# Two-layer decode attention with a feed-forward block: streaming the values past the probabilities in four column groups, and two lists of deferred steps

## The chip, the cores and the metric

The kernel runs on one core of one Trainium2 chip. The metric is device time in microseconds (us) of one execution. Before the change the median of three runs is 663.71 us (663.58 to 664.17). Matrix work is done by TensorE (PE; its weight loads are listed as PEld), elementwise work by VectorE (DVE), ScalarE (ACT) and GpSimd (POOL). SyncE (SP) issues every load from device memory (HBM). SBUF is the on-chip memory of 128 partitions, and PSUM holds the eight banks that TensorE writes into.

## The reference

One token per sequence (`Sq = 1`), four sequences, `D = 512`, 32 query heads on 8 key/value heads of `Dh = 128`, caches of `Sk = 8192` positions, bf16. The same attention and feed-forward block is applied twice, with the same weights and caches:

```python
def _A_ref(x, k_cache, v_cache, wq, wo):
    q = (x @ wq).reshape(B, 1, 32, 128).transpose(0, 2, 1, 3)
    k, v = jnp.repeat(k_cache, 4, axis=1), jnp.repeat(v_cache, 4, axis=1)
    p = softmax(einsum("bhqd,bhkd->bhqk", q, k) * 128 ** -0.5)
    o = einsum("bhqk,bhkd->bhqd", p, v)
    return o.transpose(0, 2, 1, 3).reshape(B, 1, 32 * 128) @ wo
def _B_ref(x, w_gate, w_up, w_down):
    return (silu(x @ w_gate) * (x @ w_up)) @ w_down
x = A_x
for _ in range(2):
    x = x + _A_ref(layernorm(x), ...)
    x = x + _B_ref(layernorm(x), ...)
```

A layer's K and V caches have 2 MB for each pair of sequence and key/value head, 64 such blocks of K and V together, and 128 MB in all.

## The kernel before, in words

**Units.** One unit `u` is a pair of key/value head `g = u // 4` and sequence `b = u % 4`, so there are 32 units in each layer. For a unit, four query heads (`REP = 4`) meet 8192 positions. A 2 MB block of K or V lies in one of eight slots of `kvf`: partition `p` holds positions `64 p` to `64 p + 63`, cut into eight blocks `q` of eight positions (`NB = 8`, `TB = 8`).

**Scores.** `turn` (line 389) turns each block of K in place on VectorE, as 32-bit words in 32x32 squares. `scores` (line 409) then runs four matmuls of 256 columns for each block, 32 for a unit, with the queries (`zq`) as weights. `place_q` (line 400, GpSimd) writes the next unit's queries into `zq`.

**Softmax.** Five steps follow a unit's last scores: `max_p` (line 415, VectorE), `max_t` (lines 419, 422, 425: PE, VectorE, ScalarE), `exps` (lines 431, 435, 437, 439: PE, then ScalarE), `turn_p` (line 442, VectorE: the probabilities turned into `pT`) and `total` (lines 445 and 447: the sum and its reciprocal `rl`).

**Values.** `values` runs 64 matmuls for a unit (line 495): each has 128x128 of V as weights and 32 columns of probabilities streaming past, of which the first four are wanted (the others fall into columns that nobody reads). `scale_o` (line 503) multiplies by `rl`. After the four units of a head group, `out_proj` (lines 524 to 534) applies `wo` and adds to `x`.

**What sets the order.** The program is unrolled in Python, and each engine executes its own instructions in the order in which they were written. `keys` and `values` append blocks to a list `blocks` with a nominal length each; `drain` keeps about 2 us of them waiting, so VectorE's turns are written ahead of the matmuls that need them. The steps behind softmax and values stand in one list, `line`; `advance` takes a block's nominal length off the first step's gap and writes the step down once its gap is used up. `flush(u)` writes down everything up to the last step of unit `u`. `values` puts its own `rest` (`scale_o`, then perhaps `out_proj`) in front of the list.

**Layers and loads.** Layer 0 takes units 0 to 31; layer 1 takes 29, 30, 31 first, whose K and V are still in slots 0 to 5 from layer 0 and whose K is already turned, and then 0 to 28. In a layer the order is K of a unit, then V of the unit before it; the last three V come at the end. SyncE issues loads in a fixed list (`items`), each as soon as a slot is free (`finished`, `pump`). At a layer's end the feed-forward weights `w_gate`, `w_up`, `w_down` are loaded into slots 6 and 7 and a spare strip; K and V of layer 1 can go there only when `ffn` (lines 602 and 619) has read them. `halves` reloads the slots of K of units 29 and 30 in two halves as their scores get done.

Of the kernel before, what the change touches and what calls it, by code (L numbers as in the profile page):

```python
# [5 lines left out]
ACTF = mybir.ActivationFunctionType  # L6
# [97 lines left out]
def bass_interleave_layers__gqa_block_cached__swiglu_ffn__decode_kernel(  # L104
# [24 lines left out]
    TB = 8  # L129
# [8 lines left out]
    NQ = 4  # L138
    NSLOT = 8
    NKEEP = 6  # L140
    WIDE = 32
# [4 lines left out]
    with ExitStack() as es:  # L146
# [32 lines left out]
        xx = sb("xx", [P, XB], FP32)  # L179
        lnv = sb("lnv", [P, B], FP32)  # L180
        rstd = sb("rstd", [P, B], FP32)
        xc = sb("xc", [P, XB], FP32)
        xn = sb("xn", [P, XB], BF16)
        oT = sb("oT", [P, Hq, B], BF16)
# [6 lines left out]
        pT = sb("pT", [P, 2, SW + WIDE], BF16)  # L191
        qT = pT[:, 1, 0:XQ].rearrange("p (b h) -> p b h", b=B)
        rl = sb("rl", [P, 2, REP], FP32)
        xoT = sb("xoT", [P, XB], BF16)
# [42 lines left out]
        for a in range(NA):  # L237
# [6 lines left out]
        T.op("dve", lambda e: e.memset(pT[:, :, SW:], 0.0), writes=["pT0", "pT1"])  # L244
        T.op("dve", lambda e: e.tensor_reduce(head[:], identf[:].rearrange("p (x h) -> p h x", h=REP), AX.X, ALU.max),
             reads=["ident"], writes=["head"])
        nc.scalar.preload_act_table_set("natural_log_exp_and_others")
# [4 lines left out]
        turn_of = {}  # L252

# [116 lines left out]

        def advance(us):
            if line:
                line[0][0] -= us
                while line and line[0][0] <= 0:
                    line.pop(0)[2]()

        def flush(tag=None):
            while line and (tag is None or any(s[1] == tag for s in line)):
                line.pop(0)[2]()
# [61 lines left out]
        def turn_p(u):  # L441
            T.op("dve", lambda e: e.transpose(pT[:, turn_of[u], 0:SW], pb[:]), reads=["pb"], writes=[f"pT{turn_of[u]}"])  # L442

        def total(u):
            T.op("pe", lambda e: e.matmul(bank(TOT)[:, 0:REP], lhsT=ones, rhs=rsm[:], start=True, stop=True),  # L445
                 reads=["rsm", "onesf"], writes=[f"pb{TOT}"])
            T.op("dve", lambda e: e.reciprocal(rl[:, turn_of[u], :], bank(TOT)[:, 0:REP]), reads=[f"pb{TOT}"],  # L447
                 writes=[f"rl{turn_of[u]}"])
# [35 lines left out]
        def values(L, u):  # L484
# [3 lines left out]
            def block(q):  # L488
                if q == 0:
                    flush(u)  # L490
                s = slot_of["V", L, u]

                for t in range(q * TB, (q + 1) * TB):
                    c0 = (t % TB) * QB + REP * q
                    T.op("pe", lambda e: e.matmul(bank(bk)[:, 0:WIDE], lhsT=kv[:, s, t * Dh:(t + 1) * Dh],  # L495
                                                  rhs=pT[:, turn_of[u], c0:c0 + WIDE], start=(t == 0), stop=(t == TT - 1)),
                         reads=[f"s{s}.{q}", f"pT{turn_of[u]}"], writes=[f"pb{bk}"], sig=(t % TB == TB - 1))
                if q == NB - 1:
                    finished(("V", L, u))
                    line[0:0] = rest  # L500

            def scale_o():
                T.op("dve", lambda e: e.tensor_tensor(oT[:, g * REP:(g + 1) * REP, b], bank(bk)[:, 0:REP],  # L503
                                                      rl[:, turn_of[u], :], ALU.mult),
                     reads=[f"pb{bk}", f"rl{turn_of[u]}"], writes=["oT"])

            rest = [[0.3, None, scale_o]]
# [3 lines left out]
            blocks.extend((0.2, lambda q=q: block(q)) for q in range(NB))  # L511
# [6 lines left out]
        def out_proj(g):  # L518
# [3 lines left out]
            for c in range(REP):  # L522
                for h in range(REP):
                    T.op("pe", lambda e: e.matmul(ob[h * QB:(h + 1) * QB, c, :], lhsT=pick[:, c, :],
                                                  rhs=oT[:, g * REP + h, :], start=True, stop=True),
                         reads=["oT", "ident"], writes=[f"pb{OUTB}"], sig=(h == REP - 1))
# [13 lines left out]
        def center():  # L540
# [8 lines left out]
            T.op("dve", lambda e: e.scalar_tensor_tensor(bk3(xc[:]), total, -1.0 / D, bk3(xT[:]),  # L549
                                                         op0=ALU.mult, op1=ALU.add),  # L550
                 reads=["x", f"pb{LNB}"], writes=["xc"])
            T.op("dve", lambda e: e.tensor_tensor(xx[:], xc[:], xc[:], ALU.mult), reads=["xc"], writes=["xx"])
            T.op("dve", lambda e: e.tensor_reduce(vs[:], xx[:].rearrange("p (k b) -> p b k", b=B), AX.X, ALU.add),
                 reads=["xx"], writes=["vs"])
# [147 lines left out]
```

## Time and profile before

| what | value |
| --- | --- |
| median of three runs | 663.71 us |
| the profiled execution's own time | 665.22 us |
| its span, first to last instruction | 663.3 us |
| mean granted TensorE clock | 0.816 |
| busy: PE, PEld, DVE, ACT, POOL | 509.0, 400.4, 382.7, 101.4, 19.3 us |
| moved by DMA | 275.00 MB, mean 415 GB/s |
| instructions | 17301 |

The profile's page has the busy time of each engine, the span in 40 slices, the DMA queues, the chain of work that ended last, the costliest groups of instructions (source line, engine, operation, output <- input, shapes, count, busy time, mean duration of one, and the idle time of the engine just before them with what ended it) and the DMA issues. From the trace behind it one can ask for a table of any stretches of time, and for the instructions in order of time. Clock 1.00 is TensorE at full speed. A busy share near 1 for DMA means that the mean of the 16 DMA engines had work all the time.

### The profile page before, as it was taken

How to read it: one execution, taken by the hardware profiler on the slowest of the kernel's cores; microseconds unless marked ns; L12 is line 12 of the kernel's file. 1: busy time of each engine (PE TensorE's matmuls, PEld its weight loads, DVE VectorE, ACT ScalarE, POOL GpSimd, SP SyncE). 2: the span in 40 equal slices, each digit the busy share in tenths (PEclk: the TensorE clock that was granted, in tenths of full speed). 3: DMA queues.
4: the chain of work that ended last, by engine and by line, in shares of the span. 5: the costliest groups of instructions: out<-in, count | busy, mean ns of one | idle time of the engine just before them, and what ended most of it. 6: DMA issues, size and time to landing. Idle time of an engine off the chain costs nothing.

```text
span 663.3 us, 17301 instructions
## 1 busy us (share of the span) xinstructions
PE 509.0 (77%) x7656; PEld 400.4 (60%) x7656; DVE 382.7 (58%) x897; ACT 101.4 (15%) x331; POOL 19.3 (3%) x73
## 2 busy tenths in 40 slices
PE   1767786877877777886976999878778797686796
PEld 0555565655656655665665878756556575465675
DVE  1646475575566565574732289766466566465562
ACT  0011111110111111110110212111111111011120
POOL 0000000000000000000000000000000000000000
PEclk9997788876879869788775979977788877688885
DMA  9999999999999999999998999999999999999995
GB/s 370 426 424 414 433 430 423 424 428 425 428 426 424 427 427 426 426 423 428 424 404 350 387 396 428 425 427 427 425 426 426 426 426 428 428 424 426 427 413 208
DMA packets 24107, 275.00 MB, mean 415 GB/s; under 512 B 2392, under 2 KB 2400, under 8 KB 7904
## 3 DMA queue, kind: packets, MB, share of 16 engines
q1 hardware_dynamic: 24032, 273.89, 98.2%
q8 instruction: 60, 0.98, 0.6%
q14 instruction: 15, 0.12, 0.0%
HBM read 273.88 MB, written 0.00 MB: 413 GB/s over the span
## 4 chain that ended last, share of the span: by engine, by line
DMA 68%; PE 23%; SPq 5%; DVE 2%; issue 2%; POOL 0%; DVEq 0%; POOLq 0%
DMA kvf<-in_A_k_cache_dram 63%; PE ps L409 14%; DMA kvf<-in_B_w_down_dram 5%; PE ps L495 5%; SPq L93 5%; PE ps L431 1%; PE ps L445 1%; DVE kvf L389 1%; PE ps L568 1%; DVE pT L442 0%; PE ps L419 0%; PE ps L619 0%; PE ps L530 0%; DVE rl L447 0%; PE ps L581 0%
## 5 line engine op out<-in xcount | busy, mean ns | idle before, releaser
L389 DVE STREAM_TRANSPOSE kvf<-kvf 128x512 f32<-128x512 f32 x488 | 313.1, 677 | 187.7 <-DMA kvf<-in_A_k_cache_dram 187.6
L409 PE MATMUL ps<-kvf,zq 128*128 128x256 bf16 x2048 | 332.1, 319 | 9.1 <-DVE kvf L389 6.5
L409 PEld LDWEIGHTS ps<-kvf,zq 128*128 128x128 bf16 x2048 | 215.5, 113 | 69.0 <-DVE kvf L389 10.1
L495 PEld LDWEIGHTS ps<-pT,kvf 128*128 128x128 bf16 x4096 | 119.8, 97 | 19.6 <-issue 14.3
L495 PE MATMUL ps<-pT,kvf 128*128 128x32 bf16 x4096 | 122.8, 178 | 11.4 <-DVE rl L447 9.8
L419 PE MATMUL ps<-identf,one 128*1 128x128 f32 x64 | 19.2, 301 | 100.0 <-DVE one L415 100.0
L425 ACT ACTIVATE pb<-m 1x128 f32<-1x128 f32 x64 | 19.7, 308 | 366.4 <-DVE m L422 366.4
L419 PEld LDWEIGHTS ps<-identf,one 128*1 128x1 f32 x64 | 5.2, 81 | 103.9 <-DVE one L415 103.8
L435 ACT ACTIVATE one<-ps,rstd 128x1 f32<-128x1 f32 x64 | 16.7, 262 | 136.2 <-PE ps L431 136.2
L431 PEld LDWEIGHTS ps<-one,pb 1*128 1x128 f32 x128 | 24.7, 239 | 20.2 <-issue 18.0
L437 ACT ACTIVATE pb<-ps,one,rstd 128x256 bf16<-128x256 f32 x64 | 36.1, 564 | 2.1
L400 POOL TENSOR_TENSOR zq<-scr,quad 128x64 bf16<-128x64 bf16 x62 | 18.1, 293 | 616.2 <-PE ps L409 577.4
L442 DVE STREAM_TRANSPOSE pT<-pb 128x256 bf16<-128x256 bf16 x64 | 26.5, 414 | 11.6 <-ACT pb L437 11.2
L415 DVE TENSOR_REDUCE one<-ps 128x1 f32<-128x256 f32 x64 | 25.3, 395 | 11.3 <-PE ps L409 11.1
L431 PE MATMUL ps<-one,pb 1*128 1x1 f32 x128 | 30.1, 302 | 0.3 <-ACT pb L425 0.3
L445 PEld LDWEIGHTS ps<-rsm,one 128*128 128x128 f32 x128 | 21.5, 209 | 9.0 <-ACT rsm L439 7.4
L445 PE MATMUL ps<-rsm,one 128*128 128x4 f32 x128 | 23.1, 251 | 0.7 <-ACT rsm L439 0.7
L439 ACT ACTIVATE rsm<-head,one 128x4 f32<-128x4 f32 x64 | 19.0, 297 | 2.1
L422 DVE TENSOR_REDUCE m<-ps 1x4 f32<-1x128 f32 x64 | 15.8, 247 | 5.6 <-PE ps L419 5.0
L503 DVE TENSOR_TENSOR oT<-ps,rl 128x4 bf16<-128x4 f32 x64 | 7.9, 123 | 9.3 <-PE ps L495 8.9
L530 PE MATMUL ps<-o,wo_sb 128*128 128x4 bf16 x256 | 9.2, 167 | 4.9 <-DVE o L527 4.9
L515 DVE TENSOR_TENSOR xT<-xT,ps 128x16 f32<-128x16 f32 x21 | 3.6, 171 | 15.5 <-PE ps L530 11.1
(58 smaller groups left out, 108.4 us busy)
## 6 DMA issues: line engine op xcount, KB each, us to landing
kvf<-in_A_k_cache_dram SPq DMA_DIRECT2D x60, 2048.0 KB, 31.6
kvf<-in_A_v_cache_dram SPq DMA_DIRECT2D x58, 2048.0 KB, 32.3
wq_sb<-in_A_wq_dram SPq DMA_DIRECT2D x4, 1024.0 KB, 7.6
wo_sb<-in_A_wo_dram SPq DMA_DIRECT2D x4, 1024.0 KB, 35.0
kvf<-in_A_v_cache_dram SPq DMA_DIRECT2D x8, 512.0 KB, 19.2
kvf<-in_B_w_gate_dram SPq DMA_DIRECT2D x2, 1792.0 KB, 24.3
kvf<-in_B_w_down_dram SPq DMA_DIRECT2D x4, 768.0 KB, 16.7
kvf<-in_A_v_cache_dram SPq DMA_DIRECT2D x2, 1024.0 KB, 7.0
```

The lines of the kernel that those rows point to most:

```text
L93: ins = self.eng[engname].dma_start(out_ap, in_ap)
L389: T.op("dve", lambda e: e.transpose(w, w), reads=[f"s{s}.{q}"], writes=[f"s{s}.{q}"])
L409: T.op("pe", lambda e: e.matmul(bank(bk)[:, 0:SW], lhsT=zq[:, c, z0:z0 + P], rhs=w[:, :, c // 2, :, c % 2], start=(q == 0 and c == 0), sto ...
L415: T.op("dve", lambda e: e.tensor_reduce(mx[:], bank(bk)[:, 0:SW], AX.X, ALU.max), reads=[f"pb{bk}"], writes=["mx"])
L419: T.op("pe", lambda e: e.matmul(bank(STEP)[0:1, 0:P], lhsT=mx[:], rhs=identf[:], is_transpose=True, start=True, stop=True), reads=["mx", " ...
L425: T.op("act", lambda e: e.activation(mrow.rearrange("p (x h) -> p x h", h=REP), m4[:].unsqueeze(1).to_broadcast([1, QB, REP]), ACTF.Copy), ...
L431: T.op("pe", lambda e: e.matmul(bank(STEP)[:, 0:1], lhsT=mrow, rhs=onesf[0:1, :], start=True, stop=True), reads=["pb", "onesf"], writes=[f ...
L437: T.op("act", lambda e: e.activation(pb[:], bank(bk)[:, 0:SW], ACTF.Exp, bias=nm[:], scale=by, accum_out=rs[:]), reads=[f"pb{bk}", "nm", " ...
L439: T.op("act", lambda e: e.activation(rsm[:], head[:], ACTF.Copy, scale=rs[:]), reads=["head", "rs"], writes=["rsm"])
L442: T.op("dve", lambda e: e.transpose(pT[:, turn_of[u], 0:SW], pb[:]), reads=["pb"], writes=[f"pT{turn_of[u]}"])
L445: T.op("pe", lambda e: e.matmul(bank(TOT)[:, 0:REP], lhsT=ones, rhs=rsm[:], start=True, stop=True), reads=["rsm", "onesf"], writes=[f"pb{T ...
L495: T.op("pe", lambda e: e.matmul(bank(bk)[:, 0:WIDE], lhsT=kv[:, s, t * Dh:(t + 1) * Dh], rhs=pT[:, turn_of[u], c0:c0 + WIDE], start=(t == ...
```

## The change

- For all units of a layer but its last two, the roles of the operands are swapped: 16 columns of probabilities (four blocks `q` times four heads) are the weights, and 512 columns of V (four blocks `q` times `Dh`) stream past. A unit takes 16 such matmuls in two blocks of eight. Matmul `t` writes to the 32 PSUM partitions of column group `t % 4`.
- Of each such product only the part in which both have the same `q` is wanted. A mask `own` picks it: one ScalarE activation and three VectorE instructions on 128x128 gather the wanted parts into `acc`, and one 32-bit matmul with `head` (`add_rows`) sums them and turns them, ahead of `scale_o`.
- A layer's last two units keep 64 matmuls with V as weights, but with four columns streaming in place of 32.
- The steps behind values stand in a second list, `after`; `advance` serves both lists. `values` flushes a unit's softmax steps, and of `after` up to the last step that reads the same PSUM bank.
- `rl` has three buffers in place of two, `oT` is kept for two head groups, `acc` also serves the layer norm, and two small tiles go. At the start, two PSUM banks are cleared and `own` is built.

```diff
+    NLAST = 2
+    NV = NB // 2
+        oT = sb("oT", [P, 2, REP, B], BF16)
+        acc = sb("acc", [P, Dh], FP32)
+        own = sb("own", [P, NV], FP32)
+        rl = sb("rl", [P, 3, REP], FP32)
+        T.op("dve", lambda e: e.memset(ps[:, OBK[0] * BANKF:(OBK[1] + 1) * BANKF], 0.0), ...)
...
+        after = []
         def advance(us):
+            for steps in (line, after):
+                if steps:
+                    steps[0][0] -= us
+                    while steps and steps[0][0] <= 0:
+                        steps.pop(0)[2]()
...
-                    T.op("pe", lambda e: e.matmul(bank(bk)[:, 0:WIDE], lhsT=kv[:, s, t * Dh:(t + 1) * Dh],
-                                                  rhs=pT[:, turn_of[u], c0:c0 + WIDE], start=(t == 0), stop=(t == TT - 1)), ...)
+            def begin():
+                flush(line, u)
+                flush(after, turn_of[u])
+            def end():
+                finished(("V", L, u))
+                after.extend(rest)
+            def block(i):
+                if i == 0:
+                    begin()
+                s = slot_of["V", L, u]
+                v = kv[:, s, :].rearrange("p (q t d) -> p t q d", t=TB, d=Dh)
+                for t in range(TB):
+                    j = t % NA
+                    c0 = t * QB + i * NV * REP
+                    T.op("pe", lambda e: e.matmul(bank(bk)[j * QB:j * QB + NV * REP, :],
+                                                  lhsT=pT[:, turn_of[u], c0:c0 + NV * REP], rhs=v[:, t, NV * i:NV * (i + 1), :],
+                                                  start=(i == 0 and t == j), stop=(i == 1 and t >= TB - NA)), ...)
+                if i == 1:
+                    end()
+            def own_first():
+                T.op("act", lambda e: e.activation(acc[:], bank(bk)[:, 0:Dh], ACTF.Copy, scale=own[:, 0:1]), ...)
+            def own_others():
+                for k in range(1, NV):
+                    T.op("dve", lambda e: e.scalar_tensor_tensor(acc[:], bank(bk)[:, k * Dh:(k + 1) * Dh], own[:, k:k + 1],
+                                                                 acc[:], op0=ALU.mult, op1=ALU.add), ...)
+            def add_rows():
+                T.op("pe", lambda e: e.matmul(bank(LNB)[:, 0:REP], lhsT=acc[:], rhs=head[:], start=True, stop=True), ...)
+                scale_o(LNB)
+            def block_last(q):
+                if q == 0:
+                    begin()
+                if q == NB - 2:
+                    flush(after)
+                for t in range(q * TB, (q + 1) * TB):
+                    c0 = (t % TB) * QB + REP * q
+                    T.op("pe", lambda e: e.matmul(bank(bk)[:, 0:REP], lhsT=kv[:, s, t * Dh:(t + 1) * Dh],
+                                                  rhs=pT[:, turn_of[u], c0:c0 + REP], start=(t == 0), stop=(t == TT - 1)), ...)
+            if u in unit_order[L][-NLAST:]:
+                rest = [[0.3, turn_of[u], lambda: scale_o(bk)]]
+                blocks.extend((0.25, lambda q=q: block_last(q)) for q in range(NB))
+            else:
+                rest = [[0.1, None, own_first], [0.6, turn_of[u], own_others], [1.3, None, add_rows]]
+                blocks.extend((0.5, lambda i=i: block(i)) for i in range(2))
```

## The prediction, as it was put on record

> **What bounds the kernel now.** I read the page's bars first, then its queues and its chain.
>
> ```profile
> DMA  9999999999999999999998999999999999999995
> GB/s 370 426 424 414 433 430 423 424 428 425 428 426 424 427 427 426 426 423 428 424 404 350 387 396 428 425 427 427 425 426 426 426 426 428 428 424 426 427 413 208
> q1 hardware_dynamic: 24032, 273.89, 98.2%
> q8 instruction: 60, 0.98, 0.6%
> DMA 68%; PE 23%; SPq 5%; DVE 2%; issue 2%; POOL 0%; DVEq 0%; POOLq 0%
> ```
>
> The DMA engines are full all the time but for the first slice, slices 21 to 24 and the end. At 427 GB/s the 275 MB take 644 us, 19 us under the span. So work taken off PE in the stretch that runs at 426 GB/s is worth nothing; what counts is bytes taken off the DMA, and the places where loads run dry. The table of stretches around the change of layers shows where that is (columns: length, busy time of PE, PEld, DVE, ACT, POOL, then granted clock, DMA share, GB/s):
>
> ```profile
> 364.00:366.00 2.00, 1.95 (x14) 1.30 (x12) 0.01 (x1) 0.00 (x0) 0.00 (x0) 0.81 0.85 320
> 368.00:370.00 2.00, 2.00 (x19) 1.55 (x16) 0.17 (x1) 1.36 (x5) 0.00 (x0) 1.00 0.92 328
> 390.00:392.00 2.00, 2.00 (x70) 1.95 (x68) 1.79 (x5) 0.00 (x0) 0.29 (x1) 1.00 0.96 352
> 392.00:394.00 2.00, 2.00 (x18) 1.59 (x17) 2.00 (x6) 0.72 (x3) 0.00 (x0) 1.00 0.92 328
> 394.00:396.00 2.00, 2.00 (x19) 1.58 (x18) 2.00 (x5) 0.81 (x3) 0.00 (x0) 1.00 0.98 377
> ```
>
> Two dips are PE's doing. In 364 to 372 layer 1 frees its first slots (320, 356, 328, 348 GB/s: (106+70+98+78) x 2 / 426 = 1.65 us of full rate lost). In 390 to 398 (352, 328, 377, 393) 1.2 us are lost: SyncE issued a load at 378.80, and the next only here, when PE was through the scores of unit 0:
>
> ```profile
> 390.25 0.33 SPq L93 DMA_DIRECT2D kvf<-in_A_k_cache_dram  x1
> 391.96 0.33 SPq L93 DMA_DIRECT2D kvf<-in_A_v_cache_dram  x1
> ```
>
> At both ends of a layer the feed-forward waits for weights, not for attention: PE idled 1.43 us (at 347.26) and 1.39 us (at 654.39) for `w_gate`.
>
> **The change part by part.** Durations come from these groups (last columns: busy, mean ns | idle before, releaser):
>
> ```profile
> L409 PE MATMUL ps<-kvf,zq 128*128 128x256 bf16 x2048 | 332.1, 319 | 9.1 <-DVE kvf L389 6.5
> L495 PE MATMUL ps<-pT,kvf 128*128 128x32 bf16 x4096 | 122.8, 178 | 11.4 <-DVE rl L447 9.8
> L437 ACT ACTIVATE pb<-ps,one,rstd 128x256 bf16<-128x256 f32 x64 | 36.1, 564 | 2.1
> L445 PE MATMUL ps<-rsm,one 128*128 128x4 f32 x128 | 23.1, 251 | 0.7 <-ACT rsm L439 0.7
> ```
>
> *Fewer instructions to fetch.* PE has 7656 matmuls and 7656 weight loads; at 64 bytes each that is 0.98 MB, which is what queue q8 moved in 60 packets of 16 KB. So I read q8 as PE's instruction stream. It takes 0.6% of 16 engines' 663 us: 64 us, 1.06 us a packet. The change writes 60 x 16 matmuls in place of 60 x 64 and adds 60 `add_rows`, which as 32-bit matmuls stand twice (line 445: 128 for 64 units): 7656 - 2880 + 120 = 4896, 0.63 MB, 38 packets, 22 fewer. If that time is given back evenly, 22 x 1.06 / 16 = 1.46 us; by bytes, 0.35 MB at 426 GB/s is 0.83 us; middle 1.15. VectorE and ScalarE add 182 and 60 instructions, about 15 KB or two packets on q14: 0.1 us back. I take **-1.05 us**. Bounds: 0, if the packets lie in gaps that loads don't fill; -2.6, if only nine engines carry them (the DMA share stood at 0.55 from 350 to 351, as if 9 of 16 still worked) and the last engine sets the end.
>
> *The value matmuls.* One at a time: in 390 to 420, at clock 1.00, line 409 took 19.6 us for 154, so 127 ns for 256 columns; 512 take 254 ns, 16 take 4.07 us. Line 581 tells whether column groups overlap:
>
> ```profile
> 381.88 0.57 PE L581 MATMUL ps<-pT,identf 128*32 128x112 bf16 x16 [0.37 <-DVE pT L573]
> 382.50 0.62 DVE L587 CAST scr<-ps 128x448 bf16<-128x448 f32 x1 [0.68 <-PE ps L581]
> ```
>
> These 16 go to the four column groups in turn, and their reader, the second line, started 0.62 us after the first, at a granted clock of 0.53. One at a time, 112 columns take 127 x 112/256 / 0.53 = 105 ns, 16 of them 1.68 us. So 2.7 matmuls ran side by side at least; with the last one's latency (256 ns) off, all four did. The 16 new ones then take 1.02 us at best and 1.5 at worst; I take 1.2 with `max_t`'s matmul. Now 64 matmuls with it take 1.71 us (370.86 to 372.57). So **-0.5 us** of PE for a unit, and `add_rows` gives back 0.33 (375.74 to 376.07 by line 445's place in the order): net -0.17.
>
> The Trainium skill, "TensorE: Matmul & The Clock Gate", section "Measured speedup vs the span model", has 2.38x for three column groups of 32 x 512; four at that efficiency would make 1.28 us here, an estimate from that page, and the sum less than 0.1 us worse. "TensorEngine Tiling (Array Packing)", section "Key Properties", speaks against the change: switching the tiling mode drains TensorE; line 581's 0.62 us, drain included, bounds that.
>
> *Where that counts.* From 371 on PE is busy without a break, so the order decides: values of unit 29, scores of 31, values of 30, queries, scores of 0, load. Two units' values and two `add_rows`: 2 x -0.17 = -0.35 us at 390.25; the next load, behind the values of 31, gains 0.5 more. With the dip's 1.2 us between them I take **-0.5 us**. Bounds: -1.7, if both dips' reachable part closes (1.2, and 0.5 of the first, which starts before any values run), and +5, below.
>
> *VectorE and ScalarE.* `own_first`: line 437 takes 564 ns for 256 columns, line 439 297 for 4; 128 take 0.43 us, on an engine busy 15%. `own_others`: line 587 takes 212 ns for 64 columns and 623 for 448, so 0.28 for 128, 0.85 us for three. A unit of DMA takes 9.8 us (4.19 MB at 427), VectorE has 6 us of work in it (382.7/64), so 6.9 is covered. It isn't covered from 390 to 420, where VectorE was busy 28.48 of 30 us, five units at 6.0 us each: they become 6.8 or so. But two loads are issued for each, worth 9.8 us of DMA, so the queue fills still: **0**. If the cover were gone, 0.8 us a unit.
>
> *Second list, SyncE, start.* PE's new order has `add_rows` behind 12 score matmuls, so its wait for `own_others` is covered where VectorE keeps up. SyncE's loads are the same ones in the same order: **0**. Clearing two banks and building `own` (some 1.5 us: 1024 columns at line 587's 1.07 ns each, and 0.4 for a reduce like line 245's) lies before the 4.1 us for which VectorE waits for `x`: **0**.
>
> *The ends of layers.* In layer 1, `turn_p` of unit 28 stood behind `out_proj` of group 6 (written at 647.13, its input ready at 645.7). It now goes ahead of it, but behind `own_others`, `add_rows` and `scale_o` of unit 26, and `out_proj` moves between the last unit's matmuls, where PE waits some 0.3 us for its copy (line 530's idle time at 646.45). One against the other, attention ends within 0.5 us of 653.05, and the 1.34 us to 654.39 cover it: **0**. Four columns streaming in place of 32 save nothing: line 530, with four, takes 9.2/256 = 36 ns, line 495 30.
>
> **Sum.** -1.05 - 0.5 = -1.55 us: 665.22 becomes 663.67 (span 661.75). The profiled execution was 1.51 us over the median, so 663.71 becomes **662.2 us**.
>
> **Rivals.**
> - *The fetch gives nothing back* (0.16). Its packets would slip in where the engine would pause anyway; for it, busy shares of 1.01 to 1.05 at full rate suggest slack in the counting; against it, q8 and q1 sum to 98.8%. Left are -0.5: 663.2. The Trainium skill's "Runtime: NRT & Kernel Launch", section "Instruction fetch mechanics", calls crossing a 16 KiB block mostly hidden; it speaks of the engine that fetches, not of loads beside it, and 60 packets of 16 KB agree with its size.
> - *More comes back* (0.19). Nine engines carry the fetch (-2.6), or the clock, 0.50 through most of unit 0's scores, stays at 1.00 as denser value matmuls keep PE busier, and the dip closes. -3: 660.7.
> - *No overlap* (0.08). The column groups run one after another where 512 columns come from V's strided rows. 4.07 + 0.33 against 1.7: 2.6 us more for a unit. The load at 390.25 comes 5 us later into a dry queue; in the steady stretch PE needs 6.0 + 2.6 of 9.8, so no more than that. +5 - 1 = +4: 667.7. It decides from the first value block on; line 581 speaks against it.
> - *Attention ends behind `w_gate`* (0.13). `turn_p` of unit 28 is late: VectorE, in order, has `scale_o` of 26 ahead of it, which needs `add_rows`, which stands behind 48 value matmuls of unit 27, whose V landed only at 643.3. Beyond 1.34 us each us counts in full; with 3 us more at both layers' ends 2 x 1.7, less the 1.05: +2.4, 666.1. Against it: the same steps now wait behind `out_proj`.
>
> **How the numbers follow.** My forecast has 0.44, with its own range of -1.0 to -2.2 (661.5 to 662.7). About 0.2%, 1.3 us, is what a measurement of this kernel can tell from no change: so of the 0.44, 0.29 count as faster and 0.15 as same. Faster 0.29 + 0.19 = 0.48; same 0.15 + 0.16 = 0.31; slower 0.08 + 0.13 = 0.21. The range leaves out the no-overlap case and the outer parts of the second and fourth: 660.3 to 665.2.
>
> **What would show it.** q8 with 38 packets and 0.63 MB, and full stretches through layer 0 at the same rate, so that the feed-forward of layer 0 starts 0.5 us earlier or so. The value matmuls 1.2 us or less for a unit at clock 1.00. The loads now at 390.25 and 391.96 some 0.4 and 0.9 us earlier against the feed-forward's end. `w_gate` still landing after attention at both ends. If PE shows more than 9.8 us of work for a unit, or no wait for `w_gate`, I am wrong; so I am if the time moves with q8 unchanged.

## The result, and the profile after

The changed kernel takes 660.53 us (median of four runs, 659.88 to 660.60) beside 663.94 us for the kernel before (four runs, 663.58 to 664.96). The ratio is 0.9944, with a 95% interval of 0.9927 to 0.9961: it is faster, by 3.7 us at this ratio, where 1.55 was forecast. 660.53 lies inside the forecast range; what came back was more, which is the rival that gave 660.7.

The profiled execution took 659.88 us (span 658.1), 0.65 under its median. Before's profiled execution was 1.3 over the median of its four runs, so the two traces differ by 5.3 us, and times compared between them overstate the gain. From the page of the changed kernel: the row of transfer rates, the queues, and the head of the chain that ended last.

```profile
GB/s 368 427 426 414 431 429 428 426 428 424 429 427 426 429 426 428 427 427 425 428 405 362 391 422 428 426 426 428 428 427 427 426 425 428 425 427 427 427 417 245
q1 hardware_dynamic: 24032, 273.89, 98.8%
q8 instruction: 38, 0.62, 0.4%
q14 instruction: 15, 0.12, 0.0%
DMA 64%; DVE 18%; PE 12%; SPq 5%; issue 1%; ACT 0%; POOL 0%; DVEq 0%; POOLq 0%
```

TensorE's instruction packets fell from 60 to 38. The loads are the same bytes in the same 24032 packets, and their rate in the steady stretch reads 427 as before: the row of rates doesn't show where the time went. The dip at the change of layers is one slice shorter (405, 362, 391, then 422). The groups of the new steps, from the page (last columns: busy us, mean ns | idle of the engine before them):

```profile
L517 PE MATMUL ps<-kvf,pT 128*16 128x512 bf16 x960 | 66.8, 401 | 2.1 <-DVE rl L459 2.1
L531 DVE SCALAR_TENSOR_TENSOR acc<-ps,own,acc 128x128 f32<-128x128 f32 x180 | 63.1, 351 | 6.5 <-ACT acc L526 1.9
L536 PE MATMUL ps<-head,acc 128*128 128x4 f32 x120 | 26.2, 288 | 18.9 <-DVE acc L531 18.8
L526 ACT ACTIVATE acc<-ps,own 128x128 f32<-128x128 f32 x60 | 20.6, 343 | 0.0
```

A unit's 16 value matmuls are busy for 66.8/60 = 1.11 us. One after another they would stream for 4.07 us at clock 1.00 (the prediction's figure), so four run side by side. The third row is a new wait: TensorE idles 18.8 us in all for `own_others` ahead of `add_rows`, 0.3 us a unit.

Where a layer's loads end: before, `w_up` was read in layer 0 at 351.82; now at

```profile
350.39 1.63 PE L659 MATMUL ps<-xn,kvf 128*128 128x4 bf16 x56 [2.50 <-DMA kvf<-in_B_w_up_dram]
```

That is 1.43 us earlier; the last K of layer 0 that VectorE waits for landed 2.03 us earlier (320.62 for 322.65). Between 60 and 322 us DMA is never idle in either kernel. The first turn of each unit, where VectorE's wait for a K ends, shows what happens. Three lines of the kernel before, and four of the changed kernel:

```profile
112.81 0.71 DVE L389 STREAM_TRANSPOSE kvf<-kvf 128x512 f32<-128x512 f32 x1 [3.94 <-DMA kvf<-in_A_k_cache_dram]
122.60 0.71 DVE L389 STREAM_TRANSPOSE kvf<-kvf 128x512 f32<-128x512 f32 x1 [3.31 <-DMA kvf<-in_A_k_cache_dram]
133.64 0.71 DVE L389 STREAM_TRANSPOSE kvf<-kvf 128x512 f32<-128x512 f32 x1 [4.68 <-DMA kvf<-in_A_k_cache_dram]
```

```profile
171.91 0.71 DVE L401 STREAM_TRANSPOSE kvf<-kvf 128x512 f32<-128x512 f32 x1 [2.74 <-DMA kvf<-in_A_k_cache_dram]
181.70 0.71 DVE L401 STREAM_TRANSPOSE kvf<-kvf 128x512 f32<-128x512 f32 x1 [2.80 <-DMA kvf<-in_A_k_cache_dram]
192.75 0.71 DVE L401 STREAM_TRANSPOSE kvf<-kvf 128x512 f32<-128x512 f32 x1 [4.05 <-DMA kvf<-in_A_k_cache_dram]
202.53 0.71 DVE L401 STREAM_TRANSPOSE kvf<-kvf 128x512 f32<-128x512 f32 x1 [1.87 <-DMA kvf<-in_A_k_cache_dram]
```

Landings follow each other by 9.78 us, in the changed kernel to within 0.04 and before to within 0.3, except for jumps: 122.60 to 133.64 is 11.04 and 181.70 to 192.75 is 11.05. In the first of these the DMA engines did not pause. The table of two stretches of before has a share of 1.01 and 425 GB/s (last two columns):

```profile
122.60:133.64 11.04, 7.69 (x153) 6.45 (x150) 6.29 (x15) 1.52 (x5) 0.59 (x2) 0.96 1.01 425
112.81:122.60 9.79, 7.88 (x84) 5.75 (x85) 5.80 (x14) 1.52 (x5) 0.00 (x0) 0.65 1.01 428
```

At 425 GB/s, 11.04 us are 4.69 MB, where a unit has 4.19. So most engines moved on to the next loads, while this one waited for its slowest part. The trace keeps the time at which each of a load's 16 parts was done (as many as there are DMA engines). In before, the last part of a K was done 1.8 us behind its first near 61 us, 3.1 at the first jump and 6.2 at 322.62; seven of the 16 parts are then still within 0.93 us of the first, and the other nine are 4.0 to 6.2 behind it. In the changed kernel the last part is 4.2 behind. Before has three such jumps between 60 and 322 us, 90 us apart, with 22 packets on q8; the changed kernel has one of 1.27 and two smaller ones (0.70 and 0.34), with 13 packets.

At the change of layers, the load that SyncE issued at 390.25 now goes out at 386.94 and the second dip is gone. At the end, attention now decides and not `w_gate`: the changed kernel's

```profile
649.28 0.89 PE L659 MATMUL ps<-xn,kvf 128*128 128x4 bf16 x28 [0.36 <-DVE acc L606]
```

waits for the layer norm, where before waited 1.39 us for `w_gate` at 654.39.

### The profile page after: what moved, and what is told of

Its sections match the earlier page's. It is cut to its first block, busy times and chain, and to the rows that moved or that the text cites. A ratio compares the mean times of both kernels' runs of the same rounds, so it can differ in the third digit from the quotient of the medians.

```text
span 658.1 us, 11807 instructions
## 1 busy us (share of the span) xinstructions
PE 496.4 (75%) x4896; PEld 316.7 (48%) x4896; DVE 445.6 (68%) x1079; ACT 116.5 (18%) x391; POOL 19.3 (3%) x73
## 3 DMA queue, kind: packets, MB, share of 16 engines
q1 hardware_dynamic: 24032, 273.89, 98.8%
## 4 chain that ended last, share of the span: by engine, by line
DMA 64%; DVE 18%; PE 12%; SPq 5%; issue 1%; ACT 0%; POOL 0%; DVEq 0%; POOLq 0%
DMA kvf<-in_A_k_cache_dram 59%; DVE kvf L401 12%; PE ps L421 8%; DMA kvf<-in_B_w_down_dram 5%; SPq L93 5%; DVE acc L531 3%; PE ps L517 1%; DVE pT L454 1%; PE ps L587 1%; DVE one L427 1%; DVE m L434 1%; PE ps L625 1%; PE ps L457 0%; PE ps L676 0%; PE ps L431 0%
## 5 line engine op out<-in xcount | busy, mean ns | idle before, releaser
L401 DVE STREAM_TRANSPOSE kvf<-kvf 128x512 f32<-128x512 f32 x488 | 322.4, 686 | 129.2 <-DMA kvf<-in_A_k_cache_dram 129.2
L421 PE MATMUL ps<-kvf,zq 128*128 128x256 bf16 x2048 | 343.2, 312 | 18.0 <-DVE kvf L401 14.1
L421 PEld LDWEIGHTS ps<-kvf,zq 128*128 128x128 bf16 x2048 | 209.6, 114 | 89.3 <-DVE kvf L401 39.8
L517 PE MATMUL ps<-kvf,pT 128*16 128x512 bf16 x960 | 66.8, 401 | 2.1 <-DVE rl L459 2.1
L531 DVE SCALAR_TENSOR_TENSOR acc<-ps,own,acc 128x128 f32<-128x128 f32 x180 | 63.1, 351 | 6.5 <-ACT acc L526 1.9
L536 PE MATMUL ps<-head,acc 128*128 128x4 f32 x120 | 26.2, 288 | 18.9 <-DVE acc L531 18.8
L536 PEld LDWEIGHTS ps<-head,acc 128*128 128x128 f32 x120 | 22.2, 231 | 35.8 <-DVE acc L531 35.4
L517 PEld LDWEIGHTS ps<-kvf,pT 128*16 128x16 bf16 x960 | 19.0, 90 | 33.2 <-issue 20.9
L457 PEld LDWEIGHTS ps<-rsm,one 128*128 128x128 f32 x128 | 24.8, 240 | 3.1 <-ACT rsm L451 0.9
L526 ACT ACTIVATE acc<-ps,own 128x128 f32<-128x128 f32 x60 | 20.6, 343 | 0.0
```

Of the source, the lines that this page charges most:

```text
L401: T.op("dve", lambda e: e.transpose(w, w), reads=[f"s{s}.{q}"], writes=[f"s{s}.{q}"])
L421: T.op("pe", lambda e: e.matmul(bank(bk)[:, 0:SW], lhsT=zq[:, c, z0:z0 + P], rhs=w[:, :, c // 2, :, c % 2], start=(q == 0 and c == 0), sto ...
L517: T.op("pe", lambda e: e.matmul(bank(bk)[j * QB:j * QB + NV * REP, :], lhsT=pT[:, turn_of[u], c0:c0 + NV * REP], rhs=v[:, t, NV * i:NV * ( ...
L531: T.op("dve", lambda e: e.scalar_tensor_tensor(acc[:], bank(bk)[:, k * Dh:(k + 1) * Dh], own[:, k:k + 1], acc[:], op0=ALU.mult, op1=ALU.ad ...
L536: T.op("pe", lambda e: e.matmul(bank(LNB)[:, 0:REP], lhsT=acc[:], rhs=head[:], start=True, stop=True), reads=["acc", "head"], writes=[f"pb ...
```

## The experiments

Every kernel is compared with runs of the kernel before on the same chip: medians of 664.25 for the first four kernels, 664.49 for e5 to e8, 663.62 for e9 to e12 and 664.39 for e13 to e16. So ratios are compared (the changed kernel has 0.9944), and 0.001 is 0.66 us.

### Which part gains

**e1: both lists, no streaming.** All units take the form of the last two.

```diff
-            if u in unit_order[L][-NLAST:]:
+            if True:
```

> All units of both layers keep 64 value matmuls with V as weights, with four columns streaming; the two lists and the other new tiles stay. PE has as many matmuls as before the change (7656, 60 packets on q8). Theory F (the instruction packets of PE set the time, some 0.15 us for each packet less) and theory Z (the loads that are freed earlier at the start of layer 1 set it) both expect the time before the change, 663.9 us within 0.6. If the two lists are the cause, it comes out near 660.5.

665.59 us, ratio 1.002 [1.0011, 1.003]; 60 packets; `w_up` at 351.83. The lists bring nothing by themselves. They lose 1.3 us, and near the end TensorE shows two gaps that no semaphore explains ("issue" is time in which an engine waits for nothing that the profile shows):

```profile
647.87 0.80 PE L549 MATMUL ps<-pT,kvf 128*128 128x4 bf16 x24 [1.21 <-issue]
654.07 0.59 PE L600 MATMUL ps<-xs,one 128*128 128x4 f32 x2 [1.57 <-issue]
```

**e3 and e4: streaming only in, and everywhere but in, the first five units of layer 1.** These are the units around the second dip.

```diff
+            if not (L == 1 and unit_order[L].index(u) < 5):                                        # e3
+            if u in unit_order[L][-NLAST:] or (L == 1 and unit_order[L].index(u) < 5):             # e4
```

> The values stream past the probabilities only in the first five units of layer 1; all others keep 64 matmuls with V as weights. 58 packets on q8. Theory F expects 663.3 to 663.9 us. Theory Z expects the whole gain, 660.5 to 661.5.

> The changed kernel, but the first five units of layer 1 keep 64 matmuls with V as weights too. 40 packets on q8. Theory F expects most of the gain, 660.7 to 661.7 us. Theory Z expects 663 to 664.

e3: 664.06 us, 1.0003 [0.9991, 1.0014], 58 packets. e4: 660.61 us, 0.9948 [0.9932, 0.9963], 40 packets, `w_up` at 350.36. The whole gain comes from the other units, and faster value matmuls at the dip are worth nothing that can be measured, although e3 issues the load of 390.25 at 389.25.

**e7: streaming, but with one list.** `values` puts its `rest` in front of `line` again.

```diff
-            for steps in (line, after):
+            for steps in (line,):
...
-                flush(after, turn_of[u])
...
-                after.extend(rest)
+                line[0:0] = rest
```

> The changed kernel, but the steps behind values stand in front of the softmax steps in one list, as before the change. 38 packets on q8. Theory F expects layer 0 to be as in the changed kernel (w_up at 350.4) and the end within 1 us of 660.5, later only if the softmax of the last unit, now behind the values' steps of the units before it, comes late at the end: up to 662.5. If the second list is what pays, 663 to 664.

664.57 us, 1.000 [0.9988, 1.0012]. `w_up` is read at 350.27, so layer 0 has its gain; it is lost after the change of layers. Three new steps now stand ahead of the next unit's softmax. The same stretches of the changed kernel, and then of e7:

```profile
386.00:392.00 6.00, 5.35 (x54) 3.52 (x53) 5.41 (x13) 1.77 (x6) 0.29 (x1) 1.00 1.02 423
390.00:414.00 24.00, 20.65 (x186) 12.88 (x185) 23.58 (x56) 6.07 (x21) 0.88 (x3) 1.00 1.00 427
```

```profile
386.00:392.00 6.00, 5.62 (x45) 3.41 (x43) 4.21 (x10) 1.64 (x6) 0.29 (x1) 0.77 0.84 314
390.00:414.00 24.00, 19.74 (x166) 12.35 (x165) 21.35 (x49) 5.26 (x19) 0.88 (x3) 0.93 0.97 401
```

VectorE (the fourth figure) is the bound here in the changed kernel, 23.58 of 24 us; in e7 it waits, the queue of loads runs dry (314 GB/s), and the load of 386.94 goes out at 390.17. At the end of layer 1, too, the feed-forward starts at 653.19 in place of 649.28: the last V lands 2.3 us later (646.00 for 643.70), and attention's end takes 1.6 more behind it, as the last unit's softmax now stands behind the values' steps of the units before it.

The order is not the only reason why the loads are late. At the change of layers e7 also has a gap that no semaphore explains, and its clock is 0.50 until 388.8, where the changed kernel has 1.00 from 385.0:

```profile
381.12 0.38 PE L634 MATMUL ps<-pT,identf 128*32 128x112 bf16 x7 [1.18 <-issue]
```

So e7 bounds what the order is worth by 3.7 us, and does not show it alone.

**e8: all units stream (`NLAST = 0`).**

```diff
-    NLAST = 2
+    NLAST = 0
```

> The changed kernel, with a layer's last two units streaming their values too: 4709 matmuls, 37 packets on q8. Theory F gives no more than 0.3 us for one packet less. At the end each of the last two units adds the chain of own_first, own_others and add_rows (0.34 + 1.12 + 0.4 us and their handoffs, some 2.3) behind the last V, less 0.7 of PE time: I expect 661.0 to 662.5.

664.88 us, 1.0012 [1.0, 1.0025], 37 packets. Attention's end is late in both layers, behind `add_rows`. In layer 0 that costs 0.2 us (the next layer norm's sum at 355.86 for 355.69), so the loss is in layer 1. There the feed-forward starts 10.2 us after the last V has landed (657.53 and 647.29), where the changed kernel takes 5.6 (649.28 and 643.70): the 4.6 us more match the loss against it, 0.0068 or 4.5 us. At the end of the profiled execution, which took 668.01 us, 3.1 over the median:

```profile
650.59 0.59 PE L536 MATMUL ps<-head,acc 128*128 128x4 f32 x2 [1.61 <-DVE acc L531]
654.01 0.59 PE L536 MATMUL ps<-head,acc 128*128 128x4 f32 x2 [1.30 <-DVE acc L531]
```

### Is it the packets, or TensorE's time?

**e2 and e5: pads of equal length, in many instructions or in few.** Ahead of the values of 38 units stand matmuls that nobody reads: 74 of 4 columns in e2, 8 of 512 in e5, some 2 us of TensorE each.

```diff
+                    if (12 if L else 4) <= unit_order[L].index(u) < 28:
+                        for k in range(74):
+                            T.op("pe", lambda e: e.matmul(bank(bk)[:, 0:REP], lhsT=wq_sb[:, 0, 0:P], rhs=wq_sb[:, 0, 0:REP], ...
```

> The changed kernel, with 74 matmuls of 4 columns that nobody reads ahead of the values of 38 units in the full stretches of both layers (positions 4 to 27 of layer 0, 12 to 27 of layer 1), so that PE has 7856 matmuls, 61 packets on q8, while the start of layer 1 and both ends of layers are as in the changed kernel. Theory F expects the gain gone: 663.2 to 664.2 us. Theory Z expects 660.5, within 0.5, as PE has room for 2.4 us more in each 9.8 us.

> The changed kernel, with 8 matmuls of 512 columns that nobody reads ahead of the values of the same 38 units; at clock 1.00 they take PE about the 2.0 us that the 74 narrow ones took, but PE has only 5216 matmuls, 41 packets on q8. Theory F (PE's instruction packets) expects the time of the changed kernel, 660.3 to 661.3 us. Theory P (PE's time for a unit sets when slots come free) expects the time with the 74 narrow ones, 663.0 to 664.0.

e2: 663.37 us, 0.9986 [0.9977, 0.9996], 61 packets, `w_up` at 351.93. e5: 661.75 us, 0.9966 [0.9954, 0.9977], 41 packets, `w_up` at 350.27. Same time on TensorE, and 0.002 between them. But e5 is not equal to the changed kernel either: it lacks 0.0022, 1.5 us (the two intervals just overlap). Part of that is a gap of the kind seen in e1, 0.69 us ahead of the last matmuls:

```profile
655.35 1.14 PE L681 MATMUL ps<-scr,kvf 128*128 128x4 bf16 x37 [0.69 <-issue]
```

**e16: half of e2's dose,** 37 pads for a unit.

> The changed kernel with 37 unread four-column matmuls ahead of the values of 38 units, half of e2_pad74's dose: 1406 matmuls more, 6302 in all, 11 packets of 16 KB more. TensorE has 1 us more work in a unit, and 9.8 us for it. Fetch theory: between the changed kernel (660.5) and e2_pad74 (663.4): 661.6 to 662.2, w_up read in layer 0 at 351.0 to 351.3. Rival (the pads' time on TensorE beside a clock of 0.5 makes the loss of e2_pad74, which is near TensorE's limit, and half of it stays clear of that limit): 660.5 to 660.8.

662.99 us, 0.9982 [0.9971, 0.9993], 50 packets, `w_up` at 351.41. The rival (pads cost nothing while TensorE is clear of its limit) falls. But half of the pads cost as much as all of them, so the loss is not in proportion to packets, which the fetch theory had expected. Part of it is again a gap at the end (0.31 us).

**e6: 111 pads.**

> As with 74 narrow matmuls, but 111 for each of the 38 units: 9336 matmuls, 73 packets on q8, 3.0 us more of PE for a unit. Theory F: one step of 1.2 to 1.5 us more for every 8 packets and layer than with 74, so 664.8 to 666.5 us, and w_up lands one step later in layer 0 (353.3 after 351.9 with 74 and 350.4 with none). If the packets are not the cause, the time stays at that with 74, 663.4, as PE still has room.

680.59 us, 1.0247 [1.0224, 1.0269], far beyond what was expected, and a miss of the design: TensorE itself became the bound. A stretch of 10 us, first of e2 and then of e6 (second figure: PE busy; before the last two: granted clock):

```profile
300.00:310.00 10.00, 9.03 (x141) 6.42 (x139) 7.70 (x19) 1.77 (x6) 0.29 (x1) 1.00 1.01 428
```

```profile
300.00:310.00 10.00, 10.00 (x174) 7.71 (x171) 7.16 (x16) 1.77 (x6) 0.29 (x1) 0.83 0.94 370
```

By e2's row a unit's work is some 9.8 us at full clock there, an estimate (9.03 us busy in 10, with 37 pads or 1 us more), and each stretch at clock 0.50 makes loads late. The run says nothing of the fetch.

**The landings of layer 0, over all kernels but e6.** From the first K that VectorE waits for, near 61 us, to the last, near 321, 26 more units land in each kernel, and the loads run without a pause. (The first of the 26 intervals has 12.3 to 12.5 us in every kernel, as another load of 1 MB falls into it.)

| kernels | q8 packets in it | q14 packets | length, us |
| --- | --- | --- | --- |
| before, e1, e3, e12, e2 | 22, 22, 22, 23, 26 | 6 or 7 | 261.46, 261.58, 261.57, 261.45, 261.57 |
| e16 | 19 | 7 | 260.10 |
| changed, e4, e5, e11 | 13, 13, 14, 13 | 7 | 259.23, 259.46, 259.94, 259.60 |
| e7, e8, e10 | 14, 13, 14 | 7 | 259.09, 259.23, 260.12 |
| e13, e14 | 14, 14 | 6 | 258.60, 258.83 |
| e15 | 13 | 10 | 259.58 |
| e9 | 12 | 19 | 265.48 |

With 22 or more packets on q8 it takes 261.5, with 13 or 14 (e9 apart) 259.4 in the mean, 258.6 to 260.1: 2.1 us for nine or ten packets, some 0.22 us a packet, where the forecast's price is 1.06/16 = 0.066. e5 stands with the few packets, though TensorE has e2's time.

### Does it matter whose instructions they are?

**e9: GpSimd's instructions.** 80 memsets for each of 38 units on an engine that is otherwise idle. They write into the strip of the feed-forward weights, and what this kernel computes is not the reference's block; only the times of its loads are used here.

```diff
+                    if (12 if L else 2) <= at < 26:
+                        for k in range(80):
+                            x = NSLOT * SL + 80 * at + k
+                            T.op("pool", lambda e: e.memset(kvf[:, x:x + 1], 0.0), writes=["wu"], sig=False)
```

> The changed kernel with 3040 narrow GpSimd memsets added (80 behind the placing of each of 38 units' queries: positions 2 to 25 of layer 0 and 12 to 25 of layer 1), each on a column of the spare weight strip that is overwritten before it is read. TensorE's work and its instruction stream stay as they are. Fetch theory, any engine's instructions: 3040 x 64 bytes = 0.195 MB, 12 packets of 16 KB; at 1.25 us for 8 packets +1.9 us, 662.4 us, and w_up is read in layer 0 at about 351.5 rather than 350.39 (7.5 packets by then). By bytes alone (0.195 MB at 426 GB/s): +0.46, 661.0. Rival, it is TensorE's instructions or TensorE's time that counts: 660.5, w_up at 350.4. GpSimd's memsets take about 0.1 us each, 8 of a unit's 9.8 us; if they delay the queries, TensorE waits for zq inside the steady stretch, and the run tells nothing of the fetch.

667.42 us, 1.0051 [1.0038, 1.0063], well beyond either theory. q14 rose from 15 packets to 39, of 8 KB each, and q8 stayed at 38; `w_up` is read at 356.19. Landings of K in e9:

```profile
105.03 0.71 DVE L401 STREAM_TRANSPOSE kvf<-kvf 128x512 f32<-128x512 f32 x1 [3.46 <-DMA kvf<-in_A_k_cache_dram]
115.47 0.71 DVE L401 STREAM_TRANSPOSE kvf<-kvf 128x512 f32<-128x512 f32 x1 [3.41 <-DMA kvf<-in_A_k_cache_dram]
125.27 0.71 DVE L401 STREAM_TRANSPOSE kvf<-kvf 128x512 f32<-128x512 f32 x1 [1.59 <-DMA kvf<-in_A_k_cache_dram]
135.71 0.71 DVE L401 STREAM_TRANSPOSE kvf<-kvf 128x512 f32<-128x512 f32 x1 [3.24 <-DMA kvf<-in_A_k_cache_dram]
```

Thirteen of the 26 intervals are 10.42 to 10.45 us, 0.65 more than 9.78; the memsets are spread evenly, the jumps are not, so it is not the memsets' writing that slows the loads. TensorE's work is unchanged. So a fetch delays landings, whichever engine it feeds.

**e15: a smaller dose, on a tile of its own,** 22 memsets of one byte for a unit.

> The changed kernel with 22 one-byte GpSimd memsets behind the placing of each of 38 units' queries, on a small tile of their own that nobody reads: 836 instructions, 53 KB, 6.5 packets of 8 KB, 4 of them in layer 0. TensorE, VectorE and ScalarE have the same work as in the changed kernel. Fetch theory: in layer 0 some four of the 9.78 us between landings become 10.4 (e9 showed 10.42 to 10.45), w_up is read at about 352 (350.39), and the time is 1.9 to 3 us more, 662.4 to 663.5. Rival (what e9 showed came of the strip it wrote into, or of GpSimd's 8 us a unit): 660.5 to 660.8, w_up at 350.4.

660.65 us, 0.9941 [0.9925, 0.9956], 22 packets on q14: seven more cost nothing. The fetch theory as it was put for this run (a price for each packet) falls.

**e13 and e14: fewer VectorE instructions,** K turned in pairs (e13, `n = 2`) or fours (e14) of blocks.

```diff
+            n = 4 if (10 if L else 2) <= unit_order[L].index(u) < 27 else 1
+            w = kv[:, s, q * TB * Dh:(q + n) * TB * Dh].bitcast(FP32)
```

> The changed kernel with K turned in four VectorE instructions of 1024 words a unit in place of eight of 512, for 42 units (positions 2 to 26 of layer 0, 10 to 26 of layer 1): 168 VectorE instructions fewer, 10.8 KB, 1.3 packets of 8 KB. Fetch theory, at 0.3 to 0.46 us a packet as the 24 packets of e9 cost: -0.4 to -0.6 us, 660.0. Rival (VectorE's and GpSimd's instructions cost the loads nothing): 660.5. The scores of a unit begin 0.7 us later behind its landing, which the queue of loads covers.

> As e13, with two instructions of 2048 words a unit: 252 VectorE instructions fewer, 16 KB, 2 packets of 8 KB. Fetch theory: -0.6 to -0.9 us, 659.6 to 659.9. Rival: 660.5. If the longer turns hold up the softmax steps of the unit before (VectorE is in order, and one instruction then takes 2.7 us), the loads are issued later and the time is above 660.5.

660.52 us, 0.9942 [0.9928, 0.9955], and 660.37 us, 0.9943 [0.9927, 0.9958]; 13 packets on q14 in both. The length of layer 0's landings is 0.4 to 0.6 us shorter, which the scatter allows, and the time is that of the changed kernel. The price for each packet falls here too.

What agrees with all of these is a maximum and not a sum: packets go to some of the 16 DMA engines only, a load lands with its slowest engine, and q14's packets go to another engine than q8's. Then three more on q14 by 322 us (e15, 10 for 7) stay in the shadow of q8's, and twelve more (e9, 19 for 7) stand out one by one, 0.65 us each, while q8's own jumps can no longer be seen among them. On q8 the jumps of 1.25 us after each eighth packet or so (22 packets, three jumps) say that its packets go round some eight engines.

The times of a load's 16 parts bear this out. The table has, for one execution of each kernel but e6, by how much the last part was done behind the first, for three loads: the last K of layer 0 that VectorE waits for, and the `w_down` that the feed-forward waits for last, in both layers.

| kernel | q8 packets | last K, layer 0 | `w_down`, layer 0 | `w_down`, layer 1 |
| --- | --- | --- | --- | --- |
| before | 60 | 6.2 us | 6.3 us | 7.3 us |
| e1, e3, e12 | 60, 58, 60 | 6.5, 6.6, 6.8 | 6.3, 6.4, 6.6 | 7.5, 7.3, 6.7 |
| e2 | 61 | 6.6 | 6.4 | 5.7 |
| e16 | 50 | 5.1 | 6.1 | 5.6 |
| changed | 38 | 4.2 | 4.9 | 4.9 |
| e4, e11, e13, e14, e15 | 40, then 38 | 3.4 to 4.2 | 4.4 to 4.8 | 4.9 to 5.3 |
| e5, e10 | 41 | 4.7, 5.0 | 4.9, 4.8 | 4.8, 5.1 |
| e7, e8 | 38, 37 | 3.9, 4.1 | 4.8, 4.7 | 3.9, 6.1 |
| e9 | 38 | 11.0 | 8.3 | 6.9 |

The first part of layer 0's `w_down` is done at the same time with 60 packets as with 38, 349.25 in before and 349.17 in the changed kernel; the last part is done at 355.55 and 354.08. Over both layers the last part falls behind by 3.8 us less in the changed kernel (9.8 for 13.6 us), as much as the measured gain. (The other 1.5 us by which these two traces differ lie in layer 1 ahead of the first parts, and kernels with 58 to 60 packets scatter by as much there.) e2 gives back 2.3 of the 3.8 and e16 1.9, where they lose 2.8 and 2.5 us. e5, with TensorE as busy as e2, has the changed kernel's figures. In e9 one part alone falls behind, by 11.0 us, while the other 15 stay within 4.1: so it seems that GpSimd's packets go to one engine and q8's to several. That a part is one engine's work is inferred from this; the profile names no DMA engine.

### Is it the clock?

At the start of layer 1 the scores of unit 29 ran at clock 0.50 until 364.8 in before and until 361.1 in the changed kernel, and 28 of its matmuls took 4.11 us in place of 5.16. e5 had them late again (5.48). So the clock was a rival for e5's missing 1.5 us.

**e10, e11, e12: six unread matmuls of 256 columns where TensorE waits at the start of layer 1,** in e5, in the changed kernel and in the kernel before.

```diff
+        def fill(n):
+            for _ in range(n if warm[0] else 0):
+                T.op("pe", lambda e: e.matmul(bank(OBK[0])[:, 0:SW], lhsT=wq_sb[:, 0, 0:P], rhs=wq_sb[:, 0, 0:SW], ...
```

> The kernel with 8 unread 512-column matmuls ahead of the values of 38 units (e5_wide8, 661.75 us), and six unread 256-column matmuls at the start of layer 1, where TensorE waits: two ahead of the layer norm's sum, one ahead of the queries, one ahead of their turning, two ahead of the first scores. Clock theory (part of the gain is that full clock comes back 3.4 us earlier at the start of layer 1, because the scores of unit 29 then fill the clock's step that begins near 357.5): in e5_wide8 it came back at 364.0, one step later than in the changed kernel; with the fill it comes back near 360.6, the 28 score matmuls of unit 29 take 4.1 us in place of 5.48, and the time is 660.5. Without it (the 1.2 us of e5_wide8 are the pads' own price): 661.8 to 662.0, the fill costs 0.1.

> The changed kernel with the same six unread 256-column matmuls at the start of layer 1 and nothing else. Clock theory: full clock comes back at 361.1 as it does without them, since the step before (354.3 to 357.7) holds too few of them: 660.0 to 660.6. If it comes back at 357.7, 1 us less: 659.4. Without the clock theory: 660.6.

> The kernel before with the same six unread 256-column matmuls at the start of layer 1. The instruction packets stay 60. Clock theory: the scores of unit 29 begin at 359.7, in the clock's step from 357.8 to 361.2; with the fill that step is filled for some 2.4 of 3.4 us; if that is enough, full clock comes back at 361.2 rather than 364.4, these scores take 4.1 us in place of 5.16, the loads behind them come 1 us earlier, and the ratio to before is 0.998; if it is not enough, 1.000. Fetch alone: 1.000.

In e10 the clock does what was expected. Two rows of e5, then the same two of e10 (the clock is the third figure from the end):

```profile
360.00:362.00 2.00, 2.00 (x12) 1.36 (x10) 0.00 (x0) 0.19 (x1) 0.00 (x0) 0.50 0.92 393
362.00:364.00 2.00, 2.00 (x11) 1.38 (x10) 0.00 (x0) 0.00 (x0) 0.00 (x0) 0.50 0.95 360
```

```profile
360.00:362.00 2.00, 2.00 (x17) 1.59 (x16) 0.00 (x0) 0.12 (x1) 0.00 (x0) 0.82 0.97 418
362.00:364.00 2.00, 1.50 (x15) 1.08 (x13) 0.42 (x1) 0.00 (x0) 0.29 (x1) 1.00 0.88 348
```

The 28 matmuls take 3.91 us in place of 5.48, and the loads from 366 to 375 go out 1.6 us earlier, the next, at 388.31, 0.7. The time is 661.62 us, 0.997 [0.9958, 0.9982], that of e5. e11 has 660.50 us, 0.995 [0.9938, 0.9962], with full clock back only at 362.7; e12 has 664.15 us, 1.0004 [0.9991, 1.0018]. So an earlier clock there does not reach the end, and the theory falls. e10's last matmuls have a gap of the kind of e5's:

```profile
656.21 1.29 PE L694 MATMUL ps<-scr,kvf 128*128 128x4 bf16 x43 [1.57 <-issue]
```

## Why the prediction was wrong in size

Its direction and its main cause were right. The term that carries the gain was too small, and its second term came to nothing.

- **Fewer instructions to fetch: the step that failed.** The prediction had 22 packets fewer on q8, and had exactly that, 60 to 38. It then took "22 x 1.06 / 16", "if that time is given back evenly", and settled at -1.05 us. It is not given back evenly. The row of the DMA share is a mean of 16 engines, and a load ends with its last one. In layer 0 alone nine packets fewer gave 2.2 us (259.23 for 261.46). Over both layers the last parts of loads fall behind by 3.8 us less than before. The prediction had that picture as a bound, -2.6 with "nine engines" and "the last engine sets the end", and preferred the mean. The bound was too small as well: a jump is 1.26 us and not a packet's own 1.06, and 22 packets over eight engines at 1.26 are 3.5 us, an estimate from these rows. The row that spoke against the mean was at hand: intervals of 9.78 us with three jumps to 11.04 among them, at a DMA share of 1.01.
- **The rule beside it.** The Trainium skill, "Runtime: NRT & Kernel Launch", section "Instruction fetch mechanics", has the crossing of a 16 KiB block as mostly hidden. For the engine that runs the instructions the trace of the changed kernel agrees: TensorE idles 18.0 us in all ahead of its 2048 score matmuls, 14.1 of them for VectorE's turns, and it has no gap of 0.14 us or more that no semaphore explains. For loads beside it the runs differ: nine blocks in layer 0, 2.2 us.
- **-0.5 us for the second dip: wrong, nothing came of it.** The load did move (386.94, which is 1.8 us earlier against the feed-forward's end, and 389.25 in e3), by more than the 0.4 us forecast, and the dip closed. But e3, with streaming only there, is equal to before, and e4, without it there, to the changed kernel. The prediction took a dip's 1.2 us as time at the end; e10's loads, 1.6 us earlier up to 375 and 0.7 earlier at 388, leave the time as it was.
- **The value matmuls: right.** 1.04 us from first to last at clock 1.00, 1.24 with `max_t`'s (1.2 forecast).
- **VectorE and ScalarE: sizes somewhat off, 0 right.** `own_others` takes 3 x 351 ns = 1.05 us (0.85 forecast), `own_first` 0.34 (0.43). From 390 to 414 a unit takes 7.05 us (393.98 to 401.03 to 408.08 between loads) where 6.8 was forecast; as forecast, the queue of loads fills all the same (427 GB/s). The prediction had `add_rows`' wait for `own_others` covered; it is 0.3 us a unit, on a TensorE that has time to spare.
- **Second list, 0: right against before, but not for the reason given.** The prediction weighed it as an order that costs nothing (e1's lists alone are 1.3 us slower). In e7 the three new steps, put in front of the one list, cost 0.0056, 3.7 us; the order delays the last unit's softmax by some 1.6, and the late loads it shares with a gap and a slower clock that this run happened to have.
- **The ends of layers, 0: near the edge.** The prediction said that it would be wrong if `w_gate` were no longer waited for. In layer 0 it is still waited for, 1.68 us. At the end of layer 1 it isn't: the loads came so much earlier that the cover of 1.34 us was used up, and attention's end (649.28) decides. It cost nothing that can be told: e4, which still waits 1.47 us for `w_gate`, is as fast. e8 shows what the last two units' form is worth: 0.0068, 4.5 us.

The gaps near the end can be explained, too. Over all kernels TensorE has 21 gaps of 0.14 us or more that no semaphore explains, among them e1's of 1.21 and 1.57, e5's of 0.69, e7's of 1.18, e10's of 1.57 and e16's of 0.31; before has one of 0.68 at 650.85, ahead of its wait for `w_gate`, and the changed kernel has none. In 19 of them (all but two of 0.31 in e8) TensorE starts again 1.23 to 1.60 us after a packet on q8 has ended, where packets start 3.5 us or more apart: so it waited for its own next packet. So e5 and e10 lose in part by where their packets fall. That the changed kernel has no such gap is luck, as far as the prediction goes: it put no term for it.

What stays open: the lags and gaps are read from one execution of each kernel, and 0.3 to 0.8 us of what each of e2, e5 and e16 loses is not assigned. How much of e7's loss is the order's own is not known either.

## What to carry to other kernels

In a kernel that is bound by loads, a count of instructions is a cost of its own: where the share of DMA is full, look at the intervals between landings, since a mean over 16 engines hides the one that is last. Price such a thing by the engine that is last, as a maximum over what each carries, and not by the mean. And where steps are added to a unit, look whose order they enter: with the same steps ahead of the next unit's softmax the gain was gone, at least in part by that order.

## What the hardware showed

- **Landings in steps.** 9.78 us for 4.19 MB, in the changed kernel mostly the same to 0.02 us, and then 1.25 us more at once; with packets of 8 KB for GpSimd, 0.65 us more at a time.
- **A load's parts drift apart.** At a DMA share of 1.01 a part that an instruction packet held up does not catch up: the last K of layer 0 has its last part 6.2 us behind its first in before, 4.2 in the changed kernel and 11.0 in e9.
- **TensorE can wait for its instructions.** 19 gaps of 0.16 to 1.57 us end 1.23 to 1.60 us after a packet on q8.
- **The clock moves on a grid.** Stretches at 0.50 last whole multiples of 3.41 us: 340.9 to 364.8 in before is 23.9 (seven), 340.6 to 361.1 in the changed kernel 20.5 (six), 340.2 to 360.7 in e10 20.5. The Trainium skill, "TensorE: Matmul & The Clock Gate", section "What's actually happening", has a free-running window of 3413 ns, and the traces agree.
- **Narrow matmuls seem to count little for it.** In the changed kernel's step that ended at 378.2 TensorE was never idle, but 2.6 of the 3.4 us were query matmuls of four columns, and the clock fell to 0.50 until 385.0. Six matmuls of 256 columns in the gaps before 358.3 brought it back one step earlier in e10 than in e5.
